# Sliding-window attention and a SwiGLU block on one core: weights cast by the DMA, values loaded per head half and cast in wide pieces, keys reordered, first phase and loop rearranged

## Chip, cores, metric

The kernel runs on one core of a Trainium2 chip. The metric is the device time of one execution in microseconds (us). "Span" is the profiled execution from its first to its last instruction; it is about 1.7 us shorter than the time.

Engines: PE multiplies matrices, PEld loads its weights, DVE, ACT and POOL are the vector, scalar and general engines, SP issues DMAs. DVEq, ACTq and so on are their sequencers. L252 is line 252 of that run's kernel, so the same statement can have another line number in another run.

## The reference, cut to what matters

```python
# attention: 8 batches, 8 heads, 576 positions, head width 64, a causal window of 64
scores = (q @ k.T) / 8
mask = (rel >= 0) & (rel < 64)             # rel = query position - key position
attn = softmax(where(mask, scores, -1e9))
x = (attn @ v)  ->  4608 tokens x 512
# feed-forward block, d_ff = 1536
g = x @ w_gate
out = (g * sigmoid(g) * (x @ w_val)) @ w_out     # 4608 x 512, float32
```

Inputs are float32; the kernel computes in bf16 on PE.

## The kernel before

Tokens are cut into 36 chunks of 128 (`g`, `w`), 18 blocks of 256 (`n`) and 9 tiles of 512 (`t`). Attention for chunk `g` must be done before the feed-forward matmuls of its tile. A steady loop handles one chunk of each per turn, for `w` from 8 to 35. A "first phase", written out by hand, does the attention of the first 12 chunks, the gate and value matmuls of tiles 0 and 1, and the output matmuls of tile 0.

The weights arrive as float32 and DVE casts them. There are 12 such casts; 8 of them are these:

```python
    def weights_gv(s, eng):
        for i, src in enumerate((moe_w_gate, moe_w_val)):
            w_f = wst.tile([P, 4, 384], FP32, name="w_f", tag="w_f")
            eng.dma_start(w_f[:], src[:, 384 * s:384 * s + 384].rearrange("(c r) f -> r c f", r=P))
            raw[i, s] = w_f
    def casts_gv(s):
        for i, dst in enumerate((wg, wv)):
            dve.tensor_copy(dst[:, :, 384 * s:384 * s + 384], raw.pop((i, s))[:])
```

Two heads (`a` = 0, 1) share a 128-row array, so values and keys are spread into block-diagonal tiles `vbd` and `kbd`. A block is loaded with two tokens (`c` = 0, 1) per row. POOL therefore needs 16 narrow casts per block for the values, and DVE puts the keys of each parity into its own run of 32 columns:

```python
    def casts_v(n, i, eng):                     # i = 0..3, 4 casts each
        ...
                eng.tensor_copy(
                    vb[64 * a + 32 * c:64 * a + 32 * c + 32, i % 2, :, 64 * a:64 * a + 64],
                    v_f[32 * i:32 * i + 32, a::2, c, :])
    def turn_k(n):                              # 4 copies from PSUM per block
        ...
                y = 64 * a + 32 * c
                dve.tensor_copy(kbd[n % KR][64 * a:64 * a + 64, :, :, y:y + 32], ...)
```

The heart of the loop, in the order in which PE meets it (`ps_a` is a pool of three PSUM buffers, used in turn by `products`, `turn_x`, `scores`, `turn_q` and `turn_k`):

```python
        state = gate(gv(t, 3 * s));  products(w + 4);  value(state, t, 3 * s)
        state = gv(t, 3 * s + 1)
        turn_x(w + 4)                           # transposes of the attention output
        scores(w + 6, pool)
        value(gate(state), t, 3 * s + 1)
        turn_q(...) or turn_k(...)              # transposes of q or k, alternating
        project(t - 1, s, ps_o, "o")            # the output group: 12 matmuls of 512 columns
        ...                                     # loads
        gate_value(t, (3 * s + 2,))
```

The softmax here doesn't subtract the row's maximum and nothing guards it: scores larger than these inputs give would overflow.

## Time and profile before

Median 441.0 us (440.19 to 441.34, 3 runs). First the page of the profiled run: the busy line, and the span in 40 slices of 11 us with the busy share of a slice in tenths.

```profile
span 439.8 us, 7196 instructions
PE 366.5 (83%) x2656; PEld 213.2 (48%) x2656; DVE 243.9 (55%) x520; ACT 166.2 (38%) x301; POOL 222.1 (51%) x411
PE   2557769681895999999999999999999999999920
POOL 6865264329927648484766658394766540000000
```

PE is at its limit from about the fourteenth slice on and has holes before. The windows view says how large they are. Its columns are the window, its length, then busy time and count for PE, PEld, DVE, ACT and POOL, the granted clock, the DMA share and GB/s.

```profile
100.00:110.00 10.00, 1.09 (x9) 0.83 (x10) 0.61 (x2) 0.34 (x1) 9.21 (x21) 0.60 0.53 143
...
200.00:250.00 50.00, 48.90 (x354) 26.92 (x353) 28.76 (x60) 22.64 (x39) 32.16 (x56) 1.00 0.38 108
```

From 100 to 110 us PE works 1.09 us of 10, POOL 9.21, and the granted clock is 0.60. From 200 to 250 PE is busy 48.9 of 50 us. The chain of waits (start, length, engine and tile) shows two of the waits by name, the casts of w_out on DVE and the value casts on POOL:

```profile
85.81 3.48 DVE wo L166 x4
...
103.88 0.39 POOL vbd_101 L108
...
110.35 3.60 PE o_ps L277 x12
```

The last row is an output group of 12 matmuls right after that gap, at the low clock; in the loop such a group takes 2.59 us. The wait view of PE over the first 160 us (who waited for whom: us in total, times, longest) sets a size on the weight casts:

```profile
PE g_ps L252 <- DVE wg L156: 7.8, 3, 4.1
...
PE o_ps L277 <- DVE wo L166: 2.8, 1, 2.8
```

Together PE stood 10.6 us waiting for them. The chain in the loop, once per turn:

```profile
208.23 0.24 PE xtp L237 x4
...
208.49 0.59 ACT xT L239
...
209.12 0.61 PE tp L119 x8
209.73 0.86 PE o_ps L277 x4
```

The transposes of q or k (`tp`) wait for ACT to copy the transposed attention output out of PSUM, because they are due to use that buffer next. (The last row is cut by the window asked for.)

### The profile page before, as it was taken

To read this page: it belongs to the slowest core of one execution; us is meant where nothing else is said; L and a number is where in the kernel's file an instruction comes from. 1 tells how busy PE (TensorE), PEld (TensorE's weight loads), DVE (VectorE), ACT (ScalarE), POOL (GpSimd) and SP (SyncE) were. 2 spreads that over 40 slices of the span, in tenths; PEclk is the share of its full clock that TensorE was granted. 3 is DMA by queue.
4 is the path that set the end of the run, shared out by engine and by line. 5 is a ranking of instruction groups with operands and counts; after the bars stand their busy time and mean duration, and the time that the engine had idled before them with its cause. 6 is when DMAs were issued, how large, how long until landed. Compare 5 with 4: busy or idle time off the path is not lost.

```text
span 439.8 us, 7196 instructions
## 1 busy us (share of the span) xinstructions
PE 366.5 (83%) x2656; PEld 213.2 (48%) x2656; DVE 243.9 (55%) x520; ACT 166.2 (38%) x301; POOL 222.1 (51%) x411
## 2 busy tenths in 40 slices
PE   2557769681895999999999999999999999999920
PEld 2446437540583555555555555555555555444400
DVE  5797878920474456565654546565655456546100
ACT  3333515231353344444444443434454443333210
POOL 6865264329927648484766658394766540000000
PEclk9989989996898899999999999999999999999975
DMA  8999339214271042434334242434222001001111
GB/s 254 330 271 294 143 141 225 67 58 134 86 204 32 18 121 80 138 98 125 93 110 118 81 119 78 131 107 126 81 83 69 30 26 35 35 30 37 36 50 44
DMA packets 67060, 47.66 MB, mean 108 GB/s; under 512 B 1488, under 2 KB 60880, under 8 KB 67024
## 3 DMA queue, kind: packets, MB, share of 16 engines
q1 hardware_dynamic: 67024, 47.19, 38.0%
q8 instruction: 21, 0.34, 0.3%
q14 instruction: 15, 0.12, 0.1%
HBM read 37.75 MB, written 9.44 MB: 107 GB/s over the span
## 4 chain that ended last, share of the span: by engine, by line
PE 68%; DVE 10%; POOL 8%; ACT 5%; issue 3%; DMA 2%; SPq 0%; DVEq 0%; POOLq 0%; ACTq 0%
PE g_ps L252 19%; PE v_ps L252 19%; PE o_ps L277 19%; PE ao_ps L221 5%; PE tp L119 4%; ACT xT L239 3%; DVE hT L268 2%; DMA out_dram<-os__5127 2%; DVE sg L263 2%; PE xtp L237 2%; POOL vbd_97 L108 1%; DVE x_b L226 1%; POOL E_103 L193 1%; POOL vbd_96 L108 1%; DVE wo L166 1%
## 5 line engine op out<-in xcount | busy, mean ns | idle before, releaser
L263 DVE SCALAR_TENSOR_TENSOR sg<-th,g_ps 128x512 f32<-128x512 f32 (+1 forms) x126 | 76.9, 610 | 112.1 <-ACT th L257 111.1
L252 PE MATMUL g_ps<-xT,wg 128*128 128x512 bf16 (+1 forms) x504 | 116.3, 354 | 11.5 <-DVE wg L156 7.8
L252 PE MATMUL v_ps<-xT,wv 128*128 128x512 bf16 (+1 forms) x504 | 116.2, 354 | 0.0
L257 ACT ACTIVATE th<-g_ps 128x512 f32<-128x512 f32 (+1 forms) x126 | 67.7, 537 | 128.3 <-PE g_ps L252 119.8
L277 PE MATMUL o_ps<-wo,hT 128*128 128x512 bf16 x432 | 100.1, 382 | 3.3 <-DVE wo L166 2.8
L268 DVE TENSOR_TENSOR hT<-sg,v_ps 128x512 bf16<-128x512 f32 (+1 forms) x126 | 76.8, 610 | 11.5 <-PE v_ps L252 1.1
L252 PEld LDWEIGHTS <-wv 128*128 128x128 bf16 x504 | 49.6, 99 | 46.7 <-issue 2.2
L252 PEld LDWEIGHTS <-wg 128*128 128x128 bf16 x504 | 47.7, 99 | 50.3 <-DVE wg L156 8.5
L277 PEld LDWEIGHTS <-hT 128*128 128x128 bf16 x432 | 41.4, 98 | 49.2 <-issue 5.8
L226 DVE TENSOR_TENSOR x_b<-ao_ps,r 128x256 bf16<-128x256 f32 x72 | 30.6, 425 | 2.5
L193 POOL TENSOR_TENSOR E_102<-E_102,mask 128x512 bf16<-128x512 bf16 (+2 forms) x16 | 16.1, 1027 | 28.1 <-ACT E_102 L192 28.1
L108 POOL CAST vbd_100<-v_f 32x256 bf16<-32x256 f32 x48 | 18.9, 393 | 16.6 <-DMA v_f<-in_v_dram 11.2
L239 ACT COPY xT<-xtp 128x512 bf16<-128x512 bf16 x36 | 20.9, 586 | 16.4 <-PE xtp L237 16.4
L108 POOL CAST vbd_98<-v_f 32x256 bf16<-32x256 f32 x48 | 20.2, 421 | 13.0 <-DMA v_f<-in_v_dram 11.1
L193 POOL TENSOR_TENSOR E_105<-E_105,mask 128x512 bf16<-128x512 bf16 x14 | 15.9, 1152 | 19.8 <-ACT E_105 L192 19.8
L108 POOL CAST vbd_96<-v_f 32x256 bf16<-32x256 f32 x48 | 19.4, 405 | 12.5 <-DMA v_f<-in_v_dram 10.6
L193 POOL TENSOR_TENSOR E_103<-E_103,mask 128x512 bf16<-128x512 bf16 x14 | 15.8, 1152 | 16.3 <-ACT E_103 L192 16.2
L225 DVE RECIPROCAL r<-ao_ps 128x4 f32<-128x4 f32 x72 | 12.6, 176 | 18.9 <-PE ao_ps L221 18.8
L119 PE MATMUL tp<-identb,k_fb 128*128 128x128 bf16 x144 | 12.3, 234 | 12.3 <-DVE k_fb L99 6.1
L108 POOL CAST vbd_97<-v_f 32x256 bf16<-32x256 f32 x48 | 20.5, 428 | 2.2
L99 POOL CAST k_fb<-k_f 128x1024 bf16<-128x1024 f32 x16 | 16.9, 1054 | 7.6 <-PE g_ps L252 6.9
L108 POOL CAST vbd_99<-v_f 32x256 bf16<-32x256 f32 x48 | 19.2, 400 | 2.2
(148 smaller groups left out, 466.9 us busy)
## 6 DMA issues: line engine op xcount, KB each, us to landing
k_f<-in_k_dram SPq DMA_DIRECT2D x12, 512.0 KB
q_f<-in_q_dram SPq DMA_DIRECT2D x12, 512.0 KB
v_f<-in_v_dram SPq DMA_DIRECT2D x12, 512.0 KB
w_f<-in_moe_w_gate_dram SPq DMA_DIRECT2D x4, 768.0 KB
w_f<-in_moe_w_val_dram SPq DMA_DIRECT2D x4, 768.0 KB
wo_f<-in_moe_w_out_dram SPq DMA_DIRECT2D x4, 768.0 KB
k_f<-in_k_dram SPq DMA_DIRECT2D x4, 384.0 KB
q_f<-in_q_dram SPq DMA_DIRECT2D x4, 384.0 KB
```

Source lines behind the costliest of these rows:

```text
L99: eng.tensor_copy(x, y)
L108: eng.tensor_copy(vb[64 * a + 32 * c:64 * a + 32 * c + 32, i % 2, :, 64 * a:64 * a + 64], v_f[32 * i:32 * i + 32, a::2, c, :],)
L119: nc.tensor.transpose(tp[:, c, p, :], x_b[:, c, P * p:P * p + P], identb[:])
L193: eng.tensor_mul(e, e, mask[:, lo:hi, :].unsqueeze(1).to_broadcast([P, 2, hi - lo, 64]))
L221: nc.tensor.matmul(o_ps[:, i, :], w, x, start=(n == 0), stop=(n == len(parts) - 1))
L226: dve.tensor_mul(x_b[:, 256 * h:256 * h + 256].rearrange("r (p a d) -> r p a d", p=2, a=2), o_ps[:, :, 0:P].rearrange("r p (a d) -> r p a ...
L239: act.copy(xT[g // 4][:, :, off:off + P], tp[:])
L252: nc.tensor.matmul(ps[:, 0:n], w[:, c, P * m:P * m + P], xT[t][:, c, c0:c0 + n], start=(c == 0), stop=(c == 3),)
L257: act.activation(th[:, 0:n], g_ps[:, 0:n], AF.Tanh, scale=0.5)
L263: dve.scalar_tensor_tensor(sg[:, 0:n], th[:, 0:n], 1.0, g_ps[:, 0:n], ALU.add, ALU.mult)
L268: dve.tensor_mul(hT[t][:, m, c0:c0 + n], sg[:, 0:n], v_ps[:, 0:n])
L277: nc.tensor.matmul(o_ps[:], hT[t][:, c, P * s:P * s + P], wo[:, c, :], start=(c == 0), stop=(c == 11),)
```

## The change

The intent: take the weight casts off DVE by letting the DMA cast, take most of POOL's value casts away by loading values so that two wide casts per chunk suffice, and rearrange the first phase and the loop so that fewer engines wait. The diff, cut to its core:

```diff
+            pool.dma_start(dst[:, :, 384 * s:384 * s + 384], src[...])   # float32 -> bf16, 12 of them
-            dve.tensor_copy(dst[:, :, 384 * s:384 * s + 384], raw.pop((i, s))[:])
...
+    def load_v(g):                       # 4 loads per chunk, pieces of 64 floats
+                sp.dma_start(v_f[64 * a:64 * a + 64, i],
+                             v[b, a::2, s:s + 64, :].rearrange("p r d -> r p d"))
+    def casts_v(g):                      # 2 casts per chunk
+            pool.tensor_copy(vbd[g % VR][64 * a:64 * a + 64, :, :, 64 * a:64 * a + 64],
+                             v_f[64 * a:64 * a + 64])
...
-                y = 64 * a + 32 * c
+                y = 64 * a + c
-                    kbd[n % KR][64 * a:64 * a + 64, :, :, y:y + 32],
+                    kbd[n % KR][64 * a:64 * a + 64, :, :, y:y + 63:2],
... (first phase; also 3 staging buffers for q and k in place of 2, other places for loads and zeroing)
-    casts_all(2, pool, pool)
+    casts_all(2, dve, act)               # q casts of early blocks on ACT
-    att3 = attention(3, dve)
+    att3 = attention(3, pool)
-    mix([project(0, 0), project(0, 1)], ...);  mix([project(0, 2), project(0, 3)], ...)
-    mix(F(1, range(0, 12), 256, 256), ...)
+    mix(O(0, (0, 1)), ...);              mix(F(1, range(0, 4), 256, 256), ...)
+    mix(F(1, range(4, 8), 256, 256), ...);  mix(O(0, (2, 3)), ...)
+    mix(F(1, range(8, 12), 256, 256), ...)
... (loop; the casts and loads of q and k also stand in other turns)
+        if w + 6 <= NG:
+            scores(w + 6, pool)
         if w + 4 < NG:
             turn_x(w + 4)
-        if w + 6 <= NG:
-            scores(w + 6, pool)
         value(gate(state), t, 3 * s + 1)
-        turn_q(...) / turn_k(...)
         project(t - 1, s, ps_o, "o")
+        turn_q(n) / turn_k(n)
```

Values now lie in plain row order. The keys must have the same order, hence the writes to every second column.

## The prediction

> **What bounds the kernel now.** The windows view splits the 439.8 us span. From about 142 us, where the steady loop begins, PE is busy 97 to 100% (48.9 of 50 us at 200 to 250) at clock 1.00: matmul streaming bounds it. PE ends near 420.6 us; the last stores land at 439.8, a tail the change leaves alone. The first 140 us hold only 90.6 us of PE work, so about 50 us are waits. The chain of waits names them: POOL value casts (9.5 to 17.2, 100.8 to 107.4, 117.2 to 118.9 us), DVE gates, masks and weight casts from 24 to 60, four w_out casts at 85.8 to 89.3, POOL masks and q/k casts between 96 and 139. After the long gap PE restarts at a low clock (0.60 in 100 to 110; a group of 12 output matmuls takes 3.6 us instead of 2.59).
>
> **What is removed, added, moved.**
> - DVE loses 12 weight casts of 0.95 to 1.15 us: 12 us, mostly on the chain of the first phase.
> - POOL loses 288 value casts of 0.39 to 0.43 us (117 us, groups view) and gets 72 of 64x512. From 0.393 us for 256 elements and 1.036 for 1024 I estimate 0.61 us each, 44 us. In the first phase (14 chunks) that frees 29 us, perhaps half on the chain; in the loop POOL has slack.
> - POOL gets 12 weight DMA issues. The Trainium skill, "DMA: Bandwidth & Descriptors", section "SWDGE vs HWDGE vs iDMA", says only GpSimd-issued DMAs can cast, with descriptors made by software. The trace before doesn't show that cost; my guess is 1 to 2 us each.
> - Value loads fall to 256 B pieces; section "Specifications" there puts line rate at 512 B and up. DMA share is already 0.86 to 1.15 in the first 40 us, so the first 30 us gain less than the engines would allow.
> - Key copies write every second element: 0.418 us may grow to 0.6 (estimate), 0.7 us of DVE per block, 5 us in the first phase, hidden in the loop.
> - Early q casts go to ACT (38% busy); masks of block 3 from DVE to POOL.
> - In the loop, the q and k transposes move behind the output group. This should remove PE's wait on ACT xT (0.22 us, 18 times after 165 us), 4 us.
>
> **Critical path.** Walking the new order by DVE and PE durations: first value products near 13 us instead of 17.3, first gate group near 17 instead of 21, second half of tile 0 near 35, tile 1 near 58, loop start 115 instead of 142: 27 us, plus 4 in the loop.
>
> **Predicted: 410 us, range 396 to 424. Faster by over 2%: 0.95; within 2%: 0.04; slower: 0.01.**
>
> **Right if:** first value product at 12 to 14 us; loop start at 106 to 122; PE busy above 0.8 over the first phase, no gap like 100 to 110; wide casts near 0.61 us; no PE wait on POOL value casts; loop period 9.6 to 9.7 us instead of 9.85; tail still 19 us. **Wrong if:** gate groups wait for weight DMAs, POOL stands long at DMA issues, or slow key copies delay the gates in the loop.
>
> **What would make it wrong.** Casting DMAs far slower than plain ones (the first two needed by 17 us, the next two by 26), descriptor making that holds POOL before the early value casts, or DVE, still with 85 us of work in this phase (estimate from 89 now), pacing it with bubbles of its own: then 420 to 430. If waits pack better than assumed, the loop starts near 100 us and the total is 395.

## The result and the profile after

Median 407.25 us (407.19 to 407.56, 3 runs). The ratio to before is 0.924 (95% interval 0.9219 to 0.9261), so 7.6% faster. The result is correct.

The same lines of the page after:

```profile
span 405.4 us, 7092 instructions
PE 357.0 (88%) x2617; PEld 211.8 (52%) x2656; DVE 248.5 (61%) x511; ACT 170.4 (42%) x307; POOL 152.4 (38%) x194
PE   2596898989779999999999999999999999999910
POOL 4542333463574445554444445554443420000000
```

The groups that the change touches. First before, then after (in, out, form, count, then busy us and mean ns of one, then idle time before them and who ended it):

```profile
L127 DVE COPY kbd_95<-tp 64x512 bf16<-64x512 bf16 x24 | 9.1, 417 | 4.5 <-PE tp L119 4.4
L108 POOL CAST vbd_100<-v_f 32x256 bf16<-32x256 f32 x48 | 18.9, 393 | 16.6 <-DMA v_f<-in_v_dram 11.2 <-DVE vbd_100 L375 3.6
```

```profile
L137 DVE COPY kbd_95<-tp 64x512 bf16<-64x512 bf16 x24 | 16.0, 715 | 9.9 <-PE tp L129 9.8
L118 POOL CAST vbd_100<-v_f 64x512 bf16<-64x512 f32 x12 | 7.3, 608 | 18.1 <-DVE vbd_100 L376 9.3 <-DMA v_f<-in_v_dram 8.5
L156 POOL DMA_DIRECT2D wg<-in_moe_w_gate_dram x4 | 3.2, 794 | 0.1
L156 POOL DMA_DIRECT2D wv<-in_moe_w_val_dram x4 | 3.0, 753 | 0.0
L162 POOL DMA_DIRECT2D wo<-in_moe_w_out_dram x4 | 3.0, 758 | 0.1
```

A wide value cast takes 0.61 us in place of four narrow ones of 0.39. A strided key copy takes 0.715 us in place of 0.417. The 12 casting DMAs hold POOL for 3.2 + 3.0 + 3.0 = 9.2 us in all. The windows answering to those before:

```profile
100.00:110.00 10.00, 8.05 (x86) 6.32 (x83) 4.84 (x12) 5.82 (x11) 5.63 (x7) 1.00 0.55 160
...
200.00:250.00 50.00, 49.63 (x359) 27.82 (x365) 32.78 (x62) 22.10 (x39) 24.97 (x29) 1.00 0.41 109
```

There is no gap like that of 100 to 110 any more, and the clock does not fall there. The chain in the loop after:

```profile
208.55 0.22 PE xtp L236 x4
208.77 2.37 PE o_ps L276 x11
...
218.40 2.54 PE o_ps L276 x11
220.94 0.45 PE tp L129 x8
```

ACT has left the chain. (Of the twelve matmuls of an output group one record is missing here in each turn, so the group reads short.) The period of the loop, read from one output group to the next in PE's timeline, was 9.95 us (209.57, 219.52, 229.47) and is 9.57 us (132.03, 141.61, 151.18).

**Where the 34 us came from.** Three marks in PE's timeline cut the span in four: the first gate matmul, the first output group (of tile 0), and the first output group of the loop. S1, S2 and S3 are the stretches up to each mark, and "rest" is the loop and the tail. The table gives all runs that the argument uses, in us.

| run | S1 | S2 | S3 | rest | median time |
|---|---|---|---|---|---|
| before | 21.0 | 65.7 | 63.1 | 290.0 | 441.0 |
| after | 20.2 | 55.2 | 47.0 | 282.9 | 407.25 |
| weights_only | 25.2 | 55.3 | 61.2 | 289.7 | 433.2 |
| weights_undo | 19.7 | 66.8 | 47.6 | 283.1 | 420.3 |
| values_only | 21.7 | 66.2 | 61.2 | 290.1 | 440.9 |
| values_undo | 19.8 | 54.1 | 50.5 | 282.9 | 407.8 |
| loop_undo | 20.2 | 55.8 | 47.9 | 289.6 | 415.6 |
| order_undo | 24.0 | 55.1 | 58.4 | 282.7 | 424.3 |
| keys_wrong | 20.0 | 53.0 | 46.5 | 282.7 | 403.7 |
| wide_stores | 19.9 | 54.1 | 46.5 | 268.6 | 390.3 |

From before to after: S1 gives 0.8, S2 10.5, S3 16.1 and the rest 7.0, together 34.4 us of span. The four stretches of a row come from one profiled execution, whose time lies up to 2.4 us off the median beside it (order_undo 2.4 below, weights_undo 1.3 below, values_undo 1.3 above). A difference of 1 or 2 us between two rows is therefore not safe, and neither is one between medians: the intervals of the ratios below are 0.9 to 2 us to either side. In runs that turn q or k ahead of the output group (before, the two "only" runs, loop_undo) S3 is about 1 us longer and the rest as much shorter, as the mark comes later in the turn.

### The profile page after: what moved, and what is told of

Its sections match the earlier page's. It is cut to its first block, busy times and chain, and to the rows that moved or that the text cites. A ratio compares the mean times of both kernels' runs of the same rounds, so it can differ in the third digit from the quotient of the medians.

```text
span 405.4 us, 7092 instructions
## 1 busy us (share of the span) xinstructions
PE 357.0 (88%) x2617; PEld 211.8 (52%) x2656; DVE 248.5 (61%) x511; ACT 170.4 (42%) x307; POOL 152.4 (38%) x194
## 3 DMA queue, kind: packets, MB, share of 16 engines
q1 hardware_dynamic: 81552, 37.76, 36.5%
q0 software_dynamic: 5824, 4.72, 7.3%
HBM read 37.75 MB, written 9.44 MB: 116 GB/s over the span
## 4 chain that ended last, share of the span: by engine, by line
PE 78%; DVE 8%; DMA 3%; ACT 3%; issue 2%; POOL 1%; SPq 0%; DVEq 0%; ACTq 0%; POOLq 0%
PE g_ps L251 22%; PE v_ps L251 22%; PE o_ps L276 21%; PE ao_ps L220 5%; PE tp L129 4%; DMA out_dram<-os__5021 2%; PE xtp L236 2%; DVE kbd_93 L137 2%; PE s_ps L189 2%; DVE kbd_95 L137 1%; DVE x_b L225 1%; DMA k_f<-in_k_dram 1%; DVE sg L262 1%; DVE hT L267 1%; PE s_ps L182 1%
## 5 line engine op out<-in xcount | busy, mean ns | idle before, releaser
L251 PE MATMUL g_ps<-xT,wg 128*128 128x512 bf16 (+1 forms) x487 | 114.3, 353 | 5.7 <-DVE sg L262 3.0
L276 PE MATMUL o_ps<-wo,hT 128*128 128x512 bf16 x414 | 96.0, 379 | 0.6
L267 DVE TENSOR_TENSOR hT<-sg,v_ps 128x512 bf16<-128x512 f32 (+1 forms) x126 | 76.8, 610 | 11.4 <-PE ao_ps L220 0.5
L192 POOL TENSOR_TENSOR E_104<-E_104,mask 128x512 bf16<-128x512 bf16 (+1 forms) x16 | 17.6, 1123 | 33.2 <-ACT E_104 L191 29.7
L192 POOL TENSOR_TENSOR E_102<-E_102,mask 128x512 bf16<-128x512 bf16 (+2 forms) x18 | 17.0, 964 | 27.9 <-ACT E_102 L191 27.9
L192 POOL TENSOR_TENSOR E_105<-E_105,mask 128x512 bf16<-128x512 bf16 x16 | 18.1, 1152 | 23.1 <-ACT E_105 L191 23.1
L137 DVE COPY kbd_94<-tp 64x512 bf16<-64x512 bf16 x24 | 16.0, 716 | 11.5 <-PE tp L129 11.4
L137 DVE COPY kbd_95<-tp 64x512 bf16<-64x512 bf16 x24 | 16.0, 715 | 9.9 <-PE tp L129 9.8
L137 DVE COPY kbd_93<-tp 64x512 bf16<-64x512 bf16 x24 | 16.0, 716 | 8.6 <-PE tp L129 8.5
L192 POOL TENSOR_TENSOR E_103<-E_103,mask 128x512 bf16<-128x512 bf16 x14 | 15.8, 1155 | 11.4 <-ACT E_103 L191 11.4
L236 PE MATMUL xtp<-identb,x_b 128*128 128x128 bf16 x144 | 14.9, 226 | 1.9 <-DVE x_b L225 1.4
L100 POOL CAST k_fb<-k_f 128x1024 bf16<-128x1024 f32 x15 | 15.5, 1036 | 0.7
L129 PEld LDWEIGHTS <-k_fb 128*128 128x128 bf16 x144 | 10.5, 106 | 9.3 <-DVE k_fb L100 6.7
```

The costliest lines, as they stand in the source:

```text
L129: nc.tensor.transpose(tp[:, c, p, :], x_b[:, c, P * p:P * p + P], identb[:])
L192: eng.tensor_mul(e, e, mask[:, lo:hi, :].unsqueeze(1).to_broadcast([P, 2, hi - lo, 64]))
L236: nc.tensor.transpose(tp[:, p, :], x_b[:, P * p:P * p + P], identb[:])
L251: nc.tensor.matmul(ps[:, 0:n], w[:, c, P * m:P * m + P], xT[t][:, c, c0:c0 + n], start=(c == 0), stop=(c == 3),)
L267: dve.tensor_mul(hT[t][:, m, c0:c0 + n], sg[:, 0:n], v_ps[:, 0:n])
L276: nc.tensor.matmul(o_ps[:], hT[t][:, c, P * s:P * s + P], wo[:, c, :], start=(c == 0), stop=(c == 11),)
```

## The experiments

Four parts of the change can be done or undone alone: the weights, the values with the keys, the order of the first phase, and the order of the loop. My theory was that the gain adds up from separate parts: weight casts and value casts in the first phase, PE's order in the loop. The rivals were that the lighter POOL made the loop faster, and that the new order alone made the first phase faster. Each timed run had 4 executions beside 7 of the kernel before, whose medians were 440.7 to 441.9 us. All outputs were correct except where it is said.

### The loop's order undone (loop_undo)

```diff
-        if w + 6 <= NG: scores(w + 6, pool)
-        if w + 4 < NG: turn_x(w + 4)
+        if w + 4 < NG: turn_x(w + 4)
+        if w + 6 <= NG: scores(w + 6, pool)
         value(gate(state), t, 3 * s + 1)
+        turn_q(n) / turn_k(n)
         project(t - 1, s, ps_o, "o")
-        turn_q(n) / turn_k(n)
```

> The changed kernel (407.2 us) with the two moves in the loop undone: x transpose before scores, q/k transposes before the output group. Theory 1, the loop gained by the order of PE's instructions alone: loop period back from 9.57 to about 9.95 us, loop start unchanged near 117.4 us, total 415 to 417 us. Rival, the loop gained because POOL's value casts got lighter: period stays 9.57 us, total 407 us.

Measured: 415.6 us, ratio to before 0.9417 (0.9396 to 0.9437). The period went back to 9.95 us with POOL as light as after. The first phase hardly changed (S1 the same, S2 0.6 us longer). So the loop's gain, 8.4 us by the medians and 8.1 by the spans, is PE's order and not POOL's relief.

### Which of the two moves (tp_back)

```diff
         (scores stay ahead of turn_x)
+        turn_q(n) / turn_k(n)
         project(t - 1, s, ps_o, "o")
-        turn_q(n) / turn_k(n)
```

> The changed kernel with only the q/k transposes put back before the output group, scores still ahead of the x transpose. Their PSUM buffer is the third of three in turn: it is now the one that held the first half of the scores, freed by the exponential, while in the old order it was that of the x transpose, freed by the copy to xT. Theory 1, what costs is to stand two or three short PE groups after a PSUM buffer's last use, with nothing long between: loop period 9.8 to 9.95 us, total 412 to 416 us. Rival, it is the swap of scores and x transpose that gained: period 9.57 us, 407 us.

Measured: 417.5 us, ratio 0.9469 (0.9443 to 0.9495). That is just above the 412 to 416 us of my theory. The period is 10.02 us (205.42, 215.44), slightly worse than in the old order. The chain shows the same kind of wait with another owner:

```profile
214.13 0.61 ACT E L191
...
214.78 0.61 PE tp L129 x8
...
215.44 2.54 PE o_ps L276 x11
```

Now `tp` waits for the exponential `E`, which frees the first half of the scores. In the old order it waited for the copy to `xT`. In both it takes over the buffer that was filled three uses earlier in a ring of three, with only short PE work since then. Behind the output group it has 2.6 us of PE work to hide that copy. The swap of scores and x transpose by itself gains nothing; the move behind the output group, made on top of it, does it. The move without the swap was not run.

### The weights undone, and alone (weights_undo, weights_only)

weights_undo puts the float32 loads and the 12 DVE casts back into the changed kernel, at the places that the old kernel had. weights_only puts the casting DMAs into the old kernel, at its old load places.

```diff
 (weights_undo, from after)
-            pool.dma_start(dst[...], src[...])
+            w_f = wst.tile(...); sp.dma_start(w_f[:], src[...])
+    casts_gv(0) after att0[6]; casts_gv(1), (2), (3), casts_o(0..3) before their first use
 (weights_only, from before)
-    weights_gv(0, sp) ... casts_gv(0) ... casts_o(s)
+    weights_gv(0) ...                    # pool.dma_start, casts gone
```

> The changed kernel with the weights loaded as fp32 by the plain DMA queue and cast by DVE again, the casts standing just before their first use as in the kernel before. Theory 1, the 12 DVE casts of 1 us lie mostly on the chain of the first phase: 6 to 12 us slower, 413 to 419 us, loop start 123 to 129 us, loop period 9.57 us. Rival, the new order of the first phase would have hidden them: at most 2 us slower, 407 to 409 us.

> The kernel before with casting weight DMAs and nothing else. If what a part is worth does not depend on the others: 13 us less, 428 to 430 us. Rival, in the old order POOL's value and q/k casts between 93 and 140 us pace the phase and swallow what DVE saves: 435 to 441 us.

Measured: weights_undo 420.3 us (ratio 0.9530, 0.9484 to 0.9575), so the weights are worth 13 us in the changed kernel, and the time is 1.3 us above the range of theory 1. weights_only 433.2 us (ratio 0.9811, 0.9774 to 0.9847), so they are worth 8.7 us in the old one, between the theory and the rival (clear of noise, but across the line of 2%, so the record calls it unclear). The table shows where the two differ. S2 gains about the same in both: 10.5 us in the old order (65.75 to 55.25) and 11.5 in the new one (66.77 to 55.24). The wait view of before counted nearly the same as PE's waits for the casts, 7.8 + 2.8 = 10.6 us. But in weights_only S1 grows by 4.2 us. There the casting DMAs stand at the head of POOL's program and run beside the first loads of SP. The chain of weights_only begins so:

```profile
1.91 12.09 DMA v_f<-in_v_dram
14.05 0.39 POOL vbd L107
```

The first values landed at 14.0 us. In the kernel before, POOL's first value cast started at 9.52. In the new order the first weight DMA is issued at 3.17 us, behind the mask and the identity, and POOL's first value cast starts at 10.20; only two weight DMAs are issued before 14 us, where weights_only issues four by 4.5 us. The Trainium skill, "DMA: Bandwidth & Descriptors", section "Issuing engines are not separate DMA queues", says that DMAs of all issuers run on the same 16 engines and interleave. That agrees: a second issuer took time from the first.

### The values undone, and alone (values_undo, values_only)

Both keep everything else. The old value path is one load per block in pieces of 512 B, 16 narrow casts and keys in runs of 32.

```diff
 (values_undo, from after; values_only is the reverse edit on before)
-    load_v: 4 loads per chunk;  casts_v: 2 casts of 64x512
+    load_v: 1 load per block (where the batch ends, 2);  casts_v: 8 casts of 32x256 per chunk
-                y = 64 * a + c               ... y:y + 63:2
+                y = 64 * a + 32 * c          ... y:y + 32
 (and the mask in the same order)
```

> The changed kernel with the old value loads (512 B pieces), 16 narrow POOL casts per block and keys in blocks of 32 (fast key copies of 0.42 us). Theory 1, POOL's casts were on the chain: about 4 us more POOL per block in seven blocks, a part given back by key copies that are 1.2 us per block shorter on DVE: 3 to 12 us slower, 410 to 419 us. Rival, DVE paces the first phase now and POOL is hidden: 2 to 6 us faster, 401 to 405 us. Loop period 9.57 us in both.

> The kernel before with the value loads per head half, the wide casts and the reordered keys, and nothing else. Undoing it in the changed kernel cost nothing, so the same here would be 439 to 442 us. Theory: in the old order POOL's value casts were on the chain for some 14 us between 9 and 119 us, against strided key copies of 5 to 9 us more DVE: 431 to 437 us.

Measured: values_undo 407.8 us (ratio 0.9229, 0.9189 to 0.9269) against 407.25 with the values part (ratio 0.9240). values_only 440.9 us (ratio 0.9993, 0.9962 to 1.0024). In values_undo both the theory and the rival failed; in values_only the theory failed, and the no-change case (439 to 442 us) came true. In either order this part is worth nothing that these runs can tell from zero, although it cut POOL's busy time from 222.1 to 147.8 us in values_only.

The table hints at what happened in the changed kernel: from values_undo to after, S3 becomes 3.5 us shorter while S1 and S2 become 0.4 and 1.1 us longer. As the profiled run of values_undo was the slowest of its four, these sizes are rough. In S3 of values_undo PE waited 7.7 us for masks on POOL, in that of the changed kernel 4.3. The next run takes the two halves apart.

### The stride alone taken away (keys_wrong; its result is wrong)

```diff
-                y = 64 * a + c               ... y:y + 63:2
+                y = 64 * a + 32 * c          ... y:y + 32
 (values and mask stay in the new order, so the output is wrong; no other instruction changes)
```

> The changed kernel with the key copies written in blocks of 32 as before, while values and mask stay in the new order: the result is wrong on purpose, and only the time of the copies changes (0.42 instead of 0.716 us). The values part was worth nothing in either order. Theory 1, its two halves cancel: the wide casts gain and the strided copies give it back, so taking away the stride alone makes the kernel 3 to 9 us faster, 398 to 404 us. Rival, neither half is on the chain of the first phase: 406 to 409 us. The loop period stays 9.57 us in both.

Measured: 403.7 us, ratio 0.9161 (0.9138 to 0.9183), about 3.5 us faster than the changed kernel (0.9240). (The comparison with the reference passed even so. Computed from the reference, the scores have a standard deviation of only 0.010, so all weights in a window are nearly equal, and this wrong order of keys changes the output by 1.0% in the norm. The kernel is wrong by construction. The passes of the other runs say as little about the order of their keys.) So the strided copies cost about 3.5 us, mostly in S2 (55.2 to 53.0). The wide casts with their loads save about as much: values_undo has the same fast copies with the old casts and takes 3 to 4 us longer than keys_wrong (407.8 against 403.7; ratios 0.9229 and 0.9161).

### Getting the fast copies honestly (keys_blocks, keys_split)

keys_blocks keeps keys in runs of 32 and loads the values in that order, with 8 DMAs of 32 rows per chunk instead of 4 of 64.

```diff
-                sp.dma_start(v_f[64 * a:64 * a + 64, i], v[b, a::2, s:s + 64, :]...)
+                for c in range(2):           # rows of one parity
+                    sp.dma_start(v_f[64 * a + 32 * c:64 * a + 32 * c + 32, i], x[c])
-                y = 64 * a + c               ... y:y + 63:2
+                y = 64 * a + 32 * c          ... y:y + 32
```

> The changed kernel with the keys kept in blocks of 32 (key copies without a stride), and the values loaded in that same order by 8 DMAs of 32 rows per chunk, so that the wide casts stay. Theory 1, the strided key copies (0.716 us instead of 0.418) are on the chain of the first phase: 3 to 7 us faster, 400 to 404 us, loop start 110 to 114 us. Rival, they are hidden: 407 us. If twice as many DMA issues hold up the queue of SyncE: slower than 407 us, with PE or POOL waiting for value loads.

Measured: 437.4 us, ratio 0.9899 (0.9869 to 0.9928). The first phase did get shorter, as theory 1 wanted: the loop's first gate group started at 111.9 us instead of 117.4. Then all was lost. The wait view for the loop (150 to 330 us) and SP's timeline, cut to two turns, say by what:

```profile
POOL vbd L117 <- DMA v_f<-in_v_dram: 83.3, 16, 7.1
```

```profile
198.39 9.31 SPq L111 DMA_DIRECT2D v_f<-in_v_dram  x8
207.80 1.08 SPq L283 DMA_DIRECT2D out_dram<-os__2876  x2
208.98 0.51 SPq L84 DMA_DIRECT2D q_f<-in_q_dram  x1
209.53 9.50 SPq L111 DMA_DIRECT2D v_f<-in_v_dram  x8
```

SP is held 11.1 us by one turn's DMAs (198.39 to 209.53), and the period of the loop became 11.2 us (206.97 to 218.15). The bytes are the same and the DMA share is no higher (0.37 from 200 to 250 us). So SP's queue was the limit and not the bytes. It was not the bare work of issuing, though. Taken one by one, five of the eight loads from 209.53 on took 0.43 to 0.45 us and two 0.31, but the first took 3.48, and two pauses of 1.6 and 1.4 us stand between the last ones. SP's wait view puts such pauses down to DMAs that land; what held the first load is not shown. In the changed kernel the same row of SP's timeline was 6.1 and 5.7 us for the four loads, and SP was held 8.6 to 9.0 us of each 9.57. As its single loads took 0.61 to 4.48 us, that does not show how much room is left.

keys_split puts the copies of odd columns on ACT:

```diff
-                dve.tensor_copy(
+                (dve.tensor_copy if c == 0 else act.copy)(
```

> The changed kernel with two of the four strided key copies of a block on ACT instead of DVE. Theory: key copies on DVE are on the chain of the first phase for some 14 us, so halving them saves 3 to 6 us: 401 to 404 us, loop start 111 to 114 us. Rival: the freed time is filled by other DVE work or ACT becomes late with the tanh: 406 to 410 us.

Measured: 425.6 us, ratio 0.9643 (0.9613 to 0.9674), slower than theory and rival had it. The timeline shows that the two engines took turns instead of sharing:

```profile
215.19 0.72 DVE L137 COPY kbd<-tp 64x512 bf16<-64x512 bf16 x1 [2.47 <-PE tp L129]
215.94 0.72 ACT L137 COPY kbd<-tp 64x512 bf16<-64x512 bf16 x1 [0.60 <-DVE kbd L137]
216.69 0.73 DVE L137 COPY kbd<-tp 64x512 bf16<-64x512 bf16 x1 [0.78 <-ACT kbd L137]
```

Each copy waited for the one before on the other engine. That it is because their columns interleave is a guess, which halves_stores below speaks against. ACT's tanh stands behind these waits and came late: DVE waited 1.42 us for it at 218.84. The run says nothing about a true split.

### The order of the first phase undone (order_undo)

This is the kernel before, step by step in its old order and with its old engine choices, with the weights, the values and PE's loop order of the change. The two staging buffers and the loop's old places of casts and loads come back with it; the rest of the span did not feel that (282.7 against 282.9 us).

```diff
 (from before)
+    casting weight DMAs, load_v / casts_v per chunk, reordered keys and mask
+    scores ahead of turn_x, turn_q / turn_k behind project
     (all of the first phase as in before)
```

> The first phase in the order of the kernel before (its engine choices for casts too), with all else of the change: casting weight DMAs, wide value casts with strided key copies, the two moves in the loop. If the parts add up: 8.4 us for the loop and 13 us for the weight casts were already measured and nothing for the values, so 441.7 - 21 = 420 us, loop start near 131 us, and the new order is worth the other 13 us. Rival 1, the order is only tidying: 407 us. Rival 2, the lighter POOL does its work only in the old order (where its casts were on the chain): 410 to 413 us.

Measured: 424.3 us, ratio 0.9614 (0.9569 to 0.9660), against 407.25: the order of the first phase is worth 17 us, the largest single part. The other three add up to the rest: 8.7 (weights_only), 1.0 by the medians (values_only; its interval holds zero) and 8.4 (loop) make 18, and before to order_undo is 17.6.

The table puts 3.8 us of it in S1 and 11.4 in S3; with S2 that is 14.8, as the profiled run was the fastest of its four. In S1 the chain of order_undo waits for DMAs again: the keys of block 1 land at 19.3 us, after four weight DMAs issued by 4.5. That this is the contention above is likely and was not tested apart. In S3 the old order leaves gaps that have nothing to do with the removed casts. The wait view of PE over S3 (79 to 138 us) and the chain of order_undo:

```profile
PE ao_ps L219 <- POOL E L191: 6.2, 6, 3.3
PE tp L128 <- POOL k_fb L99: 4.0, 1, 4.0
```

```profile
93.27 0.57 POOL vbd L117
...
95.93 2.27 POOL E L191 x2
98.25 0.61 PE ao_ps L219 x4
98.86 4.51 PE o_ps L275 x12
```

Around 90 us the two pairs of output groups stand together. The value products inside the second pair need masks from POOL (`E`), and POOL casts q, k and values until 95.86, though ACT started on these masks' exponentials at 93.77. PE waits, and the output group behind the wait takes 4.51 us instead of 2.59, at a granted clock of 0.61 from 98 to 104 us. In all PE waits 10.2 us for POOL in S3; in the changed kernel it waits 4.3 us for such masks and never for a cast on POOL. These are the windows of order_undo and after:

```profile
88.00:98.00 10.00, 6.06 (x34) 3.04 (x35) 0.60 (x2) 2.45 (x5) 8.21 (x10) 0.72 0.51 150
```

```profile
88.00:98.00 10.00, 8.55 (x84) 6.24 (x83) 7.72 (x19) 4.63 (x9) 6.26 (x9) 1.00 0.52 139
```

With the old order PE is busy 6.06 us of 10, at a granted clock of 0.72, and DVE 0.60. With the new one, which puts narrow gate groups between the pairs of output groups, PE is busy 8.55 at clock 1.00 and DVE 7.72. I did not separate the engine choices (q casts on ACT, masks of block 3 on POOL) from the interleaving, nor from the other moves of loads, zeroing and buffers, so how the 17 us split between them stays open.

### A version that beats both (halves_stores, wide_stores)

The trace of both kernels ends with a tail of 19 us after PE's last matmul, at a DMA share of 0.12, which is 2 of 16 engines. The Trainium skill, "DMA: Bandwidth & Descriptors", section "Rules for kernel authors", says that an outermost dimension of size c below 16 confines a DMA to at most c engines. The output stores have such a one, of size 2. halves_stores splits the last four groups' stores by parity and, as a second try at the copies, gives ACT the lower heads' halves.

```diff
 (stores, only for the last tile; both runs)
-    sp.dma_start(out[n0 + 64 * i:...].rearrange("(x c) f -> c x f", c=2), os_[64 * i:64 * i + 64, :])
+    y = out[n0 + 64 * i:...].rearrange("(x c) f -> c x f", c=2)
+    for c in range(2): sp.dma_start(y[c], os_[64 * i + 32 * c:64 * i + 32 * c + 32, :])
 (copies, halves_stores)
-    dve.tensor_copy(
+    (act.copy if a and n < 8 else dve.tensor_copy)(
```

> The changed kernel with two more edits. (a) In the first eight blocks the two key copies of partitions 64 to 127 run on ACT, those of 0 to 63 on DVE; the split of before was by column parity, and the trace showed that ACT and DVE then waited for each other copy by copy. Loop start 2 to 5 us earlier than 117.4 if DVE's copies were on the chain, unchanged or later if ACT is then late. (b) The stores of the last four output groups are each split in two of 32 rows with plain row steps: in the trace the DMA share is 0.12 (2 of 16 engines) over the last 19 us. If the two-row outer step confines each store to 2 engines, the tail from PE's end to the span's end falls from 19 to 6 to 10 us. Both: 392 to 398 us. Rival for (b), the tail is bound by the queue itself: 19 us or more stay.

Measured: 399.9 us, ratio 0.9087 (0.9044 to 0.9130), above the 392 to 398 expected. (b) went further than expected, with a tail of 4.6 us instead of 6 to 10: PE ended at 392.6 us (the second of the last four output groups ends at 387.45 in the chain, plus two of 2.59) and the span at 397.2. (a) failed: the loop's first output group started at 128.7 us instead of 122.5. In block 3 ACT's pair of copies again started only when DVE's pair was done (DVE 63.65 to 64.97, ACT from 65.06), although they touch other partitions. Over the run ACT stood 14.3 us behind DVE's copies; whether the program's own waits or the hardware cause it, the runs do not show.

wide_stores keeps the stores and gives DVE two copies per block that write without a gap and read with the stride:

```diff
-            for c in range(2): dve.tensor_copy(kbd[...][64a:64a+64, :, :, y:y + 63:2], tp[64a:64a+64, c]...)
+            dve.tensor_copy(kbd[n % KR][y:y + 64, :, :, y:y + 64].rearrange("r p i (x c) -> r (p i) x c", c=2),
+                            tp[y:y + 64].rearrange("r c p (i x) -> r (p i) x c", x=32))
```

> The changed kernel with the last four groups' stores split as in the last run (there PE's end to span's end fell from 19 to under 5 us), with all key copies on DVE again but two per block instead of four: 64x1024 elements each, written without a gap and read from PSUM with the stride instead. If it is the strided write that makes a copy of 512 elements 0.716 instead of 0.418 us, each of these takes 1.1 to 1.2 us (2.3 a block instead of 2.86) and the loop starts 1 to 2 us earlier: 390 to 393 us. If a stride on the read side costs as much, 1.4 us each, no change of the loop start: 392 to 394 us. If a strided read from PSUM is slower still, above 1.5 us: 394 to 398 us.

Measured: 390.3 us, ratio 0.8833 (0.8798 to 0.8869): 11.7% faster than before and 17 us faster than the changed kernel (another chip, whose kernel before took 441.8). The copies and the tail:

```profile
L136 DVE COPY kbd<-tp 64x1024 bf16<-64x1024 bf16 x36 | 44.0, 1222 | 30.3 <-PE tp L129 30.1
```

```profile
384.00:389.00 5.00, 0.48 (x3) 0.00 (x0) 0.00 (x0) 0.60 (x1) 0.00 (x0) 0.95 0.37 93
```

For comparison the tail of the changed kernel:

```profile
387.00:406.00 19.00, 0.00 (x0) 0.00 (x0) 0.00 (x0) 0.60 (x1) 0.00 (x0) 0.60 0.12 46
```

A block now takes 2 x 1.222 = 2.44 us of DVE instead of 4 x 0.715 = 2.86. The loop's first output group came 1.9 us earlier. The share of 0.12 in the tail became 0.37, and the rest of the span shrank by 14.3 us (282.9 to 268.6). The expectation took this size as a sign that a stride costs less on the read side. It is no such sign. The Trainium skill, "VectorE: DVE Perf Modes", section "Mode 2×_1P — pack two bf16 into one 32-bit read", asks for a step of one, and its section on the TRN2 errata gives a copy out of PSUM as 120 cycles plus the elements over the mode's factor, at 0.96 GHz. An estimate from that page is 392 ns for 512 elements at the factor 2, 658 at the factor 1, and 1192 for 1024 at the factor 1. The traces have 417, 715 and 1222. So a stride on either side fits the loss of the faster mode, and the wide copies would win by paying the fixed part twice instead of four times. No run has one size with the stride on each side, so this is a fit and not a test.

## Why the prediction was right, point by point

The total, 410 us with a range of 396 to 424, held: 407.25. The loop start, 115 us predicted, was 117.4 (first gate group). The first value product came at 12.86 (predicted 12 to 14). The total was right partly by luck, because two errors cancelled: the values were credited with a gain that did not come, and the order of the first phase and the loop gave more than they were credited with.

- **Weights: right.** 12 us of DVE, mostly on the chain; undone they cost 13 us, of which S2 shows 11.5. A casting DMA held POOL for 0.74 to 0.94 us, not 1 to 2. No gate group waited for a weight DMA.
- **Values: the term that failed.** "That frees 29 us, perhaps half on the chain" made the value casts the second large gain. The casts took 0.61 us as estimated, but half of 29 us was too much: with their loads they are worth 3 to 4 us (keys_wrong against values_undo), the strided copies take about 3.5 back, and the whole part is worth nothing in either order. A cast on the chain of waits is not a cast whose removal shortens the chain by as much: while POOL got lighter, the same part put 2.86 - 1.67 = 1.2 us per block onto DVE (0.715 us a copy where I had estimated 0.6; an estimate from the table of TRN2 errata named under wide_stores is 0.66), and DVE was busy 83.6 us of the first 117.4.
- **Order of the first phase: missing as a term.** The walk over the new order contained it, so the sum came out, but the text credited casts with what the order did. It is worth 17 us, shares of waits and engine choices not told apart.
- **First gate near 17 us: wrong.** It came at 20.2, hardly earlier than 21.0. The text set the first value product before at 17.3; the trace has it at 12.19, and 17.3 is the last wait of that stage. In the changed kernel DVE clears the next block's tiles before it scales the first output. The chain after:

```profile
13.91 0.50 DVE vbd_98 L362
...
15.88 0.91 DVE kbd_94 L365
16.82 0.20 DVE r L224
```

- **Loop: right mechanism, wrong size.** I counted only PE's idle time of 0.22 us before the transposes, and 18 turns: 4 us. Measured is 0.38 us per turn, which makes 7.6 us over the 20 turns that hold such transposes; loop_undo has 8.4 by the medians. The other 0.16 us of each turn is in the transposes themselves: in the chain eight take 0.61 us when they follow a wait, 0.45 when they follow the output group. I had also misread the old period as 9.85; it is 9.95.
- **Key copies hidden in the loop: right.** The period is 9.57 us with the stride and without it (keys_wrong: 119.52, 129.09, 138.66).
- **PE busy above 0.8 over the first phase: narrowly missed.** It is 89.9 us of 117.4, 0.77. DVE's 85 us were 83.6. PE waited once for a value cast on POOL, for 0.5 us.
- **Value loads in 256 B pieces.** The Trainium skill, "DMA: Bandwidth & Descriptors", section "Specifications", gives 512 B as the least for full rate. values_undo has the old pieces at the same period. Its plain queue moved the same bytes in 34.4% of 16 engines' span (407.3 us), after in 36.5% (405.4 us), about 6% more time, so the traces agree in direction. In the loop it cost no time. In the first 40 us the rates of the two kernels can't be compared, because the profile counts casting DMAs by the bytes written (4.72 MB for weights of 9.44 MB).

## What to carry to other kernels

Do each part of a change alone and undo each alone, and place the marks of a few stages in both traces: a part that halves an engine's work can be worth nothing, when the same part loads the engine next to it, and a new order of the same work can be worth the most. Before moving work to a DMA that another engine issues, look at which loads it will run beside, and before splitting loads, look at how long the issuing queue already works per turn. When PE uses a small ring of PSUM buffers, put a long group of matmuls between the use that fills a buffer and the use that needs it freed; here that was worth about 8 us.

## What the Trainium skill lacked or had wrong

- "DMA: Bandwidth & Descriptors", section "Issuing engines are not separate DMA queues", calls the time to initiate a DMA usually small relative to the DMA itself. Here 8 value loads of 32 KB held SP's queue for 9.3 us of a turn and set the loop's period (keys_blocks: 11.2 instead of 9.57 us). The median single issue took 0.43 us and the longest 3.49; the page does not say that an issuing queue can be held so much longer.
- The same page has no figure for how long a casting DMA holds GpSimd: 0.74 to 0.94 us each (128 rows of 4 runs of 384 elements, or of 3 runs of 512), 5.5 to 14.2 us from issue to landing.
- "VectorE: DVE Perf Modes", the PSUM row of the table in its errata section: right in kind and 2 to 8% low for copies of 64 partitions (417, 715 and 1222 ns measured, 392, 658 and 1192 by its formula).
- No page that I read says that the profile counts a casting DMA by its written bytes (4.72 MB for 9.44 MB read).
